# Attention with hashed buckets, then a channel mix: the same operations in another written sequence, on other engines

## The chip, the cores and the metric

The kernel runs on one core of a Trainium2 chip. The metric is the device time of one execution in microseconds (us). The engines are named as in the profile: PE is TensorE (matmuls; PEld its weight loads), DVE is VectorE, ACT is ScalarE, POOL is GpSimd and SP is SyncE, which here only issues transfers. Each engine works through its own queue in order and waits at semaphores for the others.

## The reference

```python
q_bits = (np.einsum('bhsd,dk->bhsk', q, proj) > 0)          # 6 sign bits for each row, k_bits alike
mask = q_bucket[:, :, :, None] == k_bucket[:, :, None, :]
scores = np.where(mask, scale * q @ k.T, -1e9)
attn = softmax(scores); x = attn @ v                        # 4 batches, 8 heads, 768 x 64
xk = mu_k * x + (1 - mu_k) * x_prev                         # x_prev: x shifted by one row; xr alike with mu_r
out = sigmoid(xr @ w_r) * (np.maximum(xk @ w_k, 0) ** 2 @ w_v)   # 512 -> 1024 -> 512
```
A row attends only to rows with the same six sign bits. The attention's output, 768 x 512 for each of four batches, goes through a gated feed-forward layer.

## The kernel before

Heads are taken in pairs: 16 pairs, numbered 0 to 15, four to a batch. In the names of operations the first number is the pair, `q` or `k` the side, and a further digit the head in the pair (0 or 1); `e` halves have one digit more.

For each pair: `ldq` loads q and k into `nat`, `ldv` loads v into `vn`. `hi` rounds q and k to fp16 (helper `scale_on`, L261 on ACT, L263 on DVE or POOL), `lo` computes what the rounding lost (L424, in the first pairs L482). `tr` transposes both by DMA (L428); pairs 0 and 1 are transposed on PE (`t`, L493) and copied out of PSUM by `evt` (L257). `bits` multiplies by the hash matrix (L448), `bx` keeps the signs as fp16 numbers (L451), and `row` copies these under the transposed q and k (L257), so that one matmul gives score plus matching bits. `sc` are the score matmuls (L566), nine steps of 1024 columns per pair; `exp` turns each into `pt` (L570, always on ACT). `va` and the three `vsum` steps (`vsum`, `b`, `c`; L379, L382, L385) prepare v and its sum over the rows. `oo` is the product with v (L593, in pairs 0 to 3 preceded by L588), `rc` and `ob` divide by the sum (L604 to L611), `ot` or `otd` transposes, `xt`, `xs`, `df` and `xk`, `xr` mix neighbouring rows (L657, L666).

Head 0 of pair 0 has a short path of its own (`add_prep_rows`): `y` transposes in fp32 on PE (L515), `ey` copies to SBUF on ACT (L257), four `hi0` roundings write q and k (two sides, two halves), `x` multiplies by the hash matrix in fp32 (L521), `ex` writes the signs (k side on ACT, L535; q side on DVE, L537).

After every fourth pair one batch of the second layer follows (`add_moe`): `kp` (L681), `relu` (L687 on ACT, L689 on DVE), `sq` (L692), `r` (L705) with `tanh` (L708), `v` (L718), `os` (L725) and the store `st`. The second layer of a batch is interleaved with the attention of later ones. Weights are loaded by `wl` and cast by `wc` (L257). `warm0` to `warm19` are matmuls on zeros (L280), and `nz` clears the rows under head 0's q and k.

All this makes 1332 operations, added in a fixed program order that gives each its dependencies. What sets the order in time is three lists at the top of the file. `ORDER` names the operations in the sequence in which their instructions are written, so it fixes the order of work inside each engine and the order of transfers on SP. `BANKS` gives each of 334 PSUM tiles its bank (eight halves of 2 KB, or four pairs for `sc` and `bits`). `ENGS` names the engine of each of the 229 operations that may run on more than one. The code only reads them:

```python
e = ENGS[self.flex] if ENGS else eng
self.slot = dict(zip(self.names, BANKS))
return [self.ops[i] for i in ORDER]
```

Of the kernel before, what the change touches and what calls it, by code (L numbers as in the profile page):

```python
# [17 lines left out]
    66, 71, 69, 1, 23, 67, 68, 22, 0, 32, 2, 29, 30, 26, 27, 24, 25, 81, 3, 4, 5, 6, 82, 31, 75, 76, 86, 84, 83, 114, 122, 88, 123, 85, 89,  # L18
    72, 87, 118, 93, 28, 33, 34, 35, 36, 37, 38, 39, 40, 41, 74, 77, 78, 79, 80, 95, 96, 99, 115, 126, 107, 70, 100, 108, 7, 8, 90, 91, 92,
    94, 97, 9, 101, 10, 11, 140, 124, 98, 102, 103, 12, 177, 119, 110, 141, 109, 127, 178, 170, 73, 171, 44, 120, 13, 179, 116, 136, 180,  # L20
    111, 104, 121, 138, 112, 137, 106, 105, 128, 181, 139, 117, 142, 129, 125, 148, 130, 230, 231, 143, 152, 149, 131, 113, 132, 134, 135,
    133, 233, 144, 234, 173, 174, 154, 155, 146, 153, 145, 147, 193, 14, 15, 156, 182, 226, 157, 205, 158, 150, 224, 223, 232, 172, 235,
    194, 206, 151, 183, 199, 45, 184, 186, 159, 203, 197, 200, 204, 276, 175, 201, 188, 283, 202, 176, 277, 185, 160, 161, 16, 187, 17, 162,
    163, 18, 189, 19, 20, 21, 279, 198, 227, 190, 191, 192, 242, 236, 284, 243, 195, 427, 426, 164, 212, 196, 237, 165, 228, 436, 437, 246,
    247, 248, 213, 249, 214, 250, 207, 244, 208, 209, 210, 251, 215, 256, 211, 216, 240, 238, 254, 229, 239, 166, 280, 245, 257, 252, 292,
    255, 285, 286, 217, 225, 491, 287, 253, 241, 218, 281, 282, 167, 42, 298, 288, 291, 290, 219, 293, 302, 169, 299, 304, 43, 168, 438,
    258, 52, 46, 48, 50, 303, 305, 278, 260, 265, 266, 261, 306, 262, 263, 220, 300, 264, 259, 439, 307, 301, 440, 296, 267, 308, 429, 289,
    441, 443, 492, 297, 47, 49, 442, 444, 309, 315, 294, 447, 316, 317, 493, 430, 268, 431, 269, 295, 449, 270, 448, 318, 319, 450, 271,
    453, 454, 445, 310, 457, 446, 432, 311, 312, 451, 459, 222, 272, 433, 273, 313, 434, 314, 458, 435, 452, 460, 463, 464, 461, 455, 465,
# [12 lines left out]
    752, 840, 896, 787, 755, 732, 407, 774, 1034, 639, 817, 812, 804, 905, 756, 805, 767, 806, 813, 768, 769, 807, 791, 414, 415, 775, 776,
    420, 820, 535, 810, 533, 793, 777, 895, 401, 792, 770, 794, 771, 800, 803, 802, 801, 821, 808, 421, 587, 588, 843, 852, 1035, 778, 842,
    811, 809, 416, 640, 641, 642, 643, 814, 815, 906, 844, 845, 422, 867, 417, 898, 907, 868, 863, 871, 423, 864, 418, 589, 424, 827, 652,
    828, 846, 847, 425, 872, 848, 897, 865, 1044, 866, 664, 653, 853, 849, 899, 654, 829, 649, 854, 665, 650, 830, 1045, 651, 655, 859, 860,
    831, 661, 861, 862, 646, 647, 656, 908, 648, 869, 877, 909, 779, 662, 887, 858, 900, 857, 856, 910, 590, 822, 870, 924, 878, 925, 928,
    879, 929, 644, 1037, 823, 824, 873, 874, 875, 658, 882, 876, 657, 880, 911, 1038, 855, 913, 881, 780, 825, 666, 1039, 1092, 1093, 920,
    667, 883, 826, 645, 663, 901, 673, 668, 669, 921, 926, 659, 674, 419, 1046, 884, 903, 927, 675, 679, 676, 677, 885, 886, 902, 930, 685,
    922, 680, 1047, 931, 923, 1090, 660, 833, 1089, 1036, 686, 687, 888, 413, 904, 1048, 1099, 781, 694, 670, 688, 671, 695, 681, 678, 689,
    672, 914, 691, 915, 1094, 1049, 1144, 1145, 912, 1052, 1051, 682, 692, 1065, 916, 1040, 937, 938, 683, 917, 918, 939, 1100, 1050, 1066,  # L50
    919, 1042, 1041, 782, 940, 690, 1043, 693, 684, 941, 832, 834, 835, 889, 696, 932, 1063, 933, 1055, 934, 1108, 1064, 1053, 1056, 836,
    935, 936, 697, 698, 1109, 1054, 700, 701, 1067, 1068, 1059, 1057, 708, 1101, 1091, 943, 1114, 1058, 702, 1102, 709, 1060, 1115, 783,
    784, 838, 837, 890, 891, 892, 944, 1151, 942, 945, 946, 1061, 1103, 1062, 1069, 703, 1112, 947, 953, 706, 1070, 1113, 707, 1124, 1152,
# [746 lines left out]
```

## Time and profile before

| | before |
|---|---|
| median of 3 runs | 246.6 us (246.0 to 246.65) |
| the profiled execution | 246.63 us, span 244.8 us |
| busy in the span | PE 231.4, DVE 202.3, ACT 183.9, POOL 77.6 us |
| costliest on ACT | 144 `exp` (L570), 139.2 us |
| costliest on DVE | 16 `lo` (L424), 26.6 us; 64 `sq` (L692), 23.6 us |
| costliest on POOL | 47 `row` copies (L257), 33.2 us |
| transfers | 43.98 MB, 180 GB/s on average |

The span is the time between the first and the last instruction of one execution; about 1.8 us lie around it. Busy time of one engine is the sum of its instructions. A matmul's end is modelled, so a busy PE can still have small gaps between starts. The number in brackets behind an idle time names who ended it.

### The profile page before, as it was taken

The page shows a single profiled execution, that of the slowest core. Times are in us where ns is not written, and L with a number is a line of the kernel's source. Part 1 is how long each engine was busy: PE and PEld are TensorE (multiplying, and loading weights), DVE is VectorE, ACT ScalarE, POOL GpSimd, SP SyncE. Part 2 cuts the span into 40 slices and gives each one's busy share as a digit, 9 for nine tenths or more (in the row PEclk, how much of TensorE's full clock was granted, in tenths as well). Part 3 has the DMA queues.
Part 4 walks back from the last instruction along what each step waited for, and adds up shares of the span by engine and source line. Part 5 has one row for each costly group of instructions (what it writes and reads, how often), then busy time and mean ns, then how long its engine had stood idle before and what let it go on. Part 6 is the DMA issues. An engine that isn't in the chain of part 4 may idle for free.

```text
span 244.8 us, 6181 instructions
## 1 busy us (share of the span) xinstructions
PE 231.4 (95%) x2472; PEld 140.2 (57%) x2472; DVE 202.3 (83%) x439; ACT 183.9 (75%) x231; POOL 77.6 (32%) x120
## 2 busy tenths in 40 slices
PE   3889799998999999999999999999999999999994
PEld 2345575665665666556557566457565674455443
DVE  2899999999998999899899999996577496677432
ACT  4799899997987999988978799785895962323321
POOL 5365458497944144213243333013010000000000
PEclk9999999999999999999999999999999999999999
DMA  7989999999899999999999458219201107121043
GB/s 219 378 199 239 250 233 172 295 276 347 312 180 241 290 326 254 222 310 248 250 258 195 108 143 176 51 54 206 75 3 32 47 0 119 45 86 43 3 171 131
DMA packets 72524, 43.98 MB, mean 180 GB/s; under 512 B 54832, under 2 KB 67504, under 8 KB 72496
## 3 DMA queue, kind: packets, MB, share of 16 engines
q1 hardware_dynamic: 72272, 43.40, 71.4%
q8 instruction: 19, 0.31, 0.5%
q10 hardware_dynamic: 224, 0.20, 0.3%
q14 instruction: 9, 0.07, 0.1%
HBM read 24.12 MB, written 6.29 MB: 124 GB/s over the span
## 4 chain that ended last, share of the span: by engine, by line
PE 71%; DVE 22%; issue 3%; ACT 1%; DMA 1%; DVEq 0%
PE ps_all L718 17%; PE ps_all L566 16%; PE ps_all L681 14%; PE ps_all L593 10%; PE ps_all L705 9%; DVE nh L424 3%; PE ps_all L448 3%; DVE a L257 3%; DVE bx L451 2%; DVE ob L611 2%; DVE xk L657 1%; DMA nat<-in_k_dram 1%; DVE k L692 1%; DVE nh L263 1%; DVE va L403 1%
## 5 line engine op out<-in xcount | busy, mean ns | idle before, releaser
L570 ACT ACTIVATE pt<-ps_all 128x1024 bf16<-128x1024 f32 x144 | 139.2, 1038 | 17.2 <-PE ps_all L566 16.2
L566 PE MATMUL ps_all<-a 128*128 128x256 f16 (+1 forms) x384 | 80.5, 325 | 3.1 <-DVE bx L451 0.9
L257 POOL COPY a<-bx 6x384 f32<-6x384 f32 x47 | 33.2, 706 | 67.3 <-DVE bx L451 44.2
L593 PEld LDWEIGHTS <-pt 128*128 128x128 bf16 x1152 | 43.6, 97 | 12.6 <-issue 4.2
L681 PE MATMUL ps_all<-xk,wk 128*128 128x384 bf16 x256 | 49.4, 326 | 0.4 <-DVE kr L689 0.4
L566 PEld LDWEIGHTS <-a 128*128 128x128 f16 x384 | 33.8, 97 | 25.3 <-issue 4.6
L593 PE MATMUL ps_all<-va,pt 128*128 128x65 bf16 x1152 | 46.2, 193 | 1.3 <-DVE xt L257 1.2
L718 PE MATMUL ps_all<-wv,k 128*128 128x512 bf16 (+2 forms) x208 | 47.2, 363 | 0.0
L681 PEld LDWEIGHTS <-wk 128*128 128x128 bf16 x256 | 24.1, 98 | 16.6 <-issue 1.4
L687 ACT ACTIVATE kr<-ps_all 128x384 bf16<-128x384 f32 x41 | 19.5, 500 | 16.0 <-PE ps_all L681 12.2
L718 PEld LDWEIGHTS <-k 128*128 128x128 bf16 x208 | 19.4, 98 | 19.3 <-issue 0.3
L708 ACT ACTIVATE rs<-ps_all 128x512 f32<-128x512 f32 x24 | 14.1, 600 | 18.5 <-PE ps_all L705 10.4
L692 DVE TENSOR_TENSOR k<-kr 128x384 bf16<-128x384 bf16 x64 | 23.6, 389 | 3.9 <-ACT kr L687 3.6
L424 DVE SCALAR_TENSOR_TENSOR nh<-nat,nh 128x1536 f16<-128x1536 f32 (+1 forms) x16 | 26.6, 1663 | 0.1
L725 DVE SCALAR_TENSOR_TENSOR os<-rs,ps_all 128x512 f32<-128x512 f32 (+2 forms) x26 | 16.7, 640 | 11.0 <-PE ps_all L718 10.2
L705 PE MATMUL ps_all<-wr,xr 128*128 128x512 bf16 x96 | 24.5, 379 | 0.0
L611 DVE TENSOR_TENSOR ob<-ps_all,rc 128x384 bf16<-128x384 f32 x32 | 17.4, 551 | 0.4
L451 DVE TENSOR_SCALAR bx<-ps_all 128x768 uint16<-128x768 uint16 (+1 forms) x16 | 15.2, 950 | 3.1 <-PE ps_all L448 3.0
L689 DVE TENSOR_SCALAR kr<-ps_all 128x384 bf16<-128x384 f32 x23 | 12.6, 549 | 4.9 <-PE ps_all L681 4.8
L403 DVE SCALAR_TENSOR_TENSOR va<-ps_all,vn 128x384 bf16<-128x384 f32 x24 | 12.5, 547 | 3.3 <-PE ps_all L398 2.2
L705 PEld LDWEIGHTS <-xr 128*128 128x128 bf16 x96 | 9.1, 98 | 9.4 <-issue 0.3
L448 PE MATMUL ps_all<-a,p 128*32 128x512 f16 (+1 forms) x248 | 13.3, 328 | 0.0
(90 smaller groups left out, 200.5 us busy)
## 6 DMA issues: line engine op xcount, KB each, us to landing
vn<-in_v_dram SPq DMA_DIRECT2D x16, 384.0 KB, 5.0
out_dram<-os SPq DMA_DIRECT2D x23, 256.0 KB, 2.2
nat<-in_q_dram SPq DMA_DIRECT2D x15, 384.0 KB, 5.0
nat<-in_k_dram SPq DMA_DIRECT2D x15, 384.0 KB, 5.2
wst<-in_moe_w_k_dram SPq DMA_DIRECT2D x2, 512.0 KB, 6.0
wst<-in_moe_w_r_dram SPq DMA_DIRECT2D x2, 512.0 KB, 5.4
wst<-in_moe_w_v_dram SPq DMA_DIRECT2D x2, 512.0 KB, 5.6
os<-in_moe_w_k_dram SPq DMA_DIRECT2D x1, 512.0 KB, 4.2
```

Source lines behind the costliest of these rows:

```text
L257: nc.scalar.copy(o, i_) if e == "ACT" else tt_on(e).tensor_copy(o, i_)
L424: nc.vector.scalar_tensor_tensor(out=nh[:, :, D:P], in0=nat.rearrange("p j (c d) -> p (j c) d", d=D), scalar=QS, in1=nh[:, :, 0:D], op0=AL ...
L448: nc.tensor.matmul(ps[32 * i : 32 * i + 32, lo:hi], w_, side_a[side][sa][:, j, lo:hi], start=st, stop=not st)
L451: nc.vector.tensor_scalar(out=bx_t[sx][0:rows].bitcast(U16), in0=ps_t[plan.slot[nm]][0:rows, 0:S].bitcast(U16).rearrange("p (c e) -> p c e ...
L566: nc.tensor.matmul(ps[:, lo - s * STEP : hi - s * STEP], side_a["k"][sa][:, j, jc * P : (jc + 1) * P], side_a["q"][sa][:, j, q0 : q0 + hi ...
L570: nc.scalar.activation(out=pt_t[sp][:, s * STEP : (s + 1) * STEP], in_=ps_t[plan.slot[nm]], func=AF.Exp, bias=EBIAS, scale=ESC)
L593: nc.tensor.matmul(oo[:, ic * 65 : ic * 65 + 65], pt_t[sp][:, o : o + P], va_t[sa][:, j, jc, 0 : D + 1], start=(not uc and ic == 0 and jc ...
L611: nc.vector.tensor_tensor(out=ob_t[so][:, :, j * D : (j + 1) * D], in0=oo[:, :, 0:D], in1=rc_t[sr][:, 1, :].unsqueeze(2).to_broadcast([P, ...
L681: nc.tensor.matmul(ps[:, 0:HALF], wk_sb[:, d, fc * P : (fc + 1) * P], xk_t[mx[d]][:, h * HALF : (h + 1) * HALF], start=(d == 0), stop=(d = ...
L692: nc.vector.tensor_tensor(out=k2_t[s2][:, h * HALF : (h + 1) * HALF], in0=kr_t[sk], in1=kr_t[sk], op=ALU.mult)
L705: nc.tensor.matmul(sm(nr), xr_t[mx[d]][:, c * P : (c + 1) * P], wr_sb[:, d, :], start=(d == 0), stop=(d == NDC - 1))
L718: nc.tensor.matmul(sm(nv)[:, x0:x1], k2_t[(b * NFC + fc) % NK2][:, c * P : (c + 1) * P], wv_sb[:, fc, x0:x1], start=(fc == 0), stop=(fc == ...
```

## The change

No operation is added, removed or resized. The three lists are replaced: `ORDER` by another permutation of the same 1332 numbers, `BANKS` differs in 156 of 334 places, `ENGS` in 80 of 229 places. The moves between engines are:

| operation | from | to | which |
|---|---|---|---|
| rounding of head 0 | POOL | ACT | `hi0q00` (so all four are on ACT) |
| `hi` | ACT | DVE | `hi1k0`, `hi9`, `hi11`, `hi14` |
| `evt` | DVE | ACT | `evt1k1` |
| `nz` | DVE | POOL | `nz0q0` |
| `va` | POOL | DVE | `va1`, `va2` |
| `vsum` | POOL to DVE, 13 | DVE to POOL, 10 | e.g. `vsum1`, `vsum6` with b and c to DVE; `vsum1c`, `vsum12` to POOL |
| `row` | POOL to DVE, 7 | DVE to POOL, 9 | e.g. `row1k1` to DVE; `row2q1`, `row2k1` to POOL |
| `relu` | ACT to DVE, 13 | DVE to ACT, 16 | |
| `wc` | | | `wc6` DVE to POOL, `wc7` POOL to ACT, `wc8` POOL to DVE |

In the first head the written sequence on each engine becomes:

| engine | before | after |
|---|---|---|
| PE | `warm0`, `y0k0`, `warm1` to `4`, `x0k0`, `y0q0`, two warm-ups, `x0q0` | `warm0` to `13`, `y0q0`, `y0k0`, `x0q0`, `x0k0` |
| ACT | `ey0k0`, `hi0k01`, `hi0k00`, `ex0k00`, `ey0q0`, `ex0k01`, `hi1k0`, `hi0q01`, `hi1k1`, `evt0q1`, `evt0k1`, `va0`, `exp0_2` | `ey0q0`, `hi0q01`, `ey0k0`, `hi0q00`, `hi0k00`, `hi0k01`, `ex0k00`, `hi1k1`, `ex0k01`, `evt0k1`, `evt0q1`, `exp0_2`, `va0` |
| DVE | `hi1q0`, `hi1q1`, `lo1q1`, `hi0q1`, `lo0q1`, `hi0k1`, `lo1q0`, `lo0k1`, `ex0q00`, `ex0q01` | `hi1q0`, `hi1q1`, `lo1q0`, `lo1q1`, `hi0k1`, `lo0k1`, `hi0q1`, `ex0q00`, `lo0q1`, `ex0q01` |

On SP the first loads stay in place; `ldv1` moves ahead of `ldq3`, `ldv2` from the ninth place behind the second `tr2`, `mur` from before `tr2` to behind `tr3`, and `ldv5` from before `tr6` to behind `wl7`. From 20 us on, neighbours change places on every engine by a few positions, in the last fifth by up to 19 positions on DVE. The bank of `oo0_1` was freed by `ob0` and is now one that `bx1` frees.

```diff
 ORDER = [
-    66, 71, 69, 1, 23, 67, 68, 22, 0, 32, 2, 29, 30, 26, 27, 24, 25, 81, 3, 4, 5, 6, 82, 31, 75, 76, 86, 84, 83, 114, 122, 88, 123, 85, 89,
+    1, 23, 29, 30, 26, 27, 24, 68, 25, 22, 28, 33, 34, 35, 36, 37, 0, 32, 38, 39, 31, 75, 76, 2, 3, 4, 5, 6, 7, 8, 9, 10, 11, 12, 13, 14,
+    15, 66, 71, 69, 67, 72, 107, 114, 122, 88, 115, 123, 99, 100, 81, 89, 93, 82, 91, 84, 90, 95, 92, 96, 94, 40, 41, 74, 77, 78, 79, 80,
...
 BANKS = [
-    3, 6, 0, 5, 2, 1, 7, 0, 6, 7, 2, 7, 3, 2, 0, 2, 2, 0, 3, 0, 0, 2, 2, 2, 6, 2, 2, 3, 2, 2, 0, 3, 3, 2, 3, 6, 7, 5, 0, 1, 0, 0, 1, 2, 0,
+    2, 6, 7, 7, 5, 1, 6, 0, 3, 2, 7, 6, 1, 2, 0, 2, 2, 0, 3, 3, 0, 2, 3, 2, 7, 2, 2, 3, 2, 2, 0, 3, 3, 0, 3, 6, 7, 1, 0, 1, 0, 0, 1, 2, 2,
...
 ENGS = [
-    "DVE", "DVE", "POOL", "POOL", "POOL", "POOL", "POOL", "POOL", "DVE", "POOL", "POOL", "ACT", "ACT", "ACT", "ACT", "ACT", "POOL", "ACT",
-    "DVE", "ACT", "DVE", "ACT", "POOL", "POOL", "ACT", "POOL", "POOL", "POOL", "DVE", "DVE", "ACT", "DVE", "DVE", "DVE", "ACT", "DVE",
+    "POOL", "DVE", "POOL", "POOL", "POOL", "POOL", "POOL", "POOL", "POOL", "ACT", "DVE", "ACT", "ACT", "ACT", "ACT", "ACT", "ACT", "ACT",
+    "DVE", "ACT", "DVE", "ACT", "POOL", "POOL", "ACT", "POOL", "POOL", "POOL", "DVE", "DVE", "DVE", "DVE", "DVE", "DVE", "ACT", "ACT",
...
```

22 lines of the change are left out of this document (11 added, 11 removed), and 115 rows, old and new, of tables (BANKS, ORDER).

## The prediction

> **What bounds the kernel now.** I read the page's busy shares first, then the busy time by stretch, then the chain that ended last, then the timeline where that chain changes engine.
>
> ```profile
> PE 231.4 (95%) x2472; PEld 140.2 (57%) x2472; DVE 202.3 (83%) x439; ACT 183.9 (75%) x231; POOL 77.6 (32%) x120
> ```
> ```profile
> 0.00:13.00 13.00, 8.32 (x47) 4.26 (x49) 7.55 (x19) 8.15 (x15) 5.25 (x31) 1.00 0.89 302
> 13.00:62.00 49.00, 44.49 (x655) 29.62 (x650) 47.95 (x78) 45.58 (x50) 33.31 (x37) 1.00 1.04 252
> 62.00:165.00 103.00, 101.98 (x1098) 61.91 (x1097) 98.52 (x218) 91.84 (x113) 35.61 (x47) 1.00 0.90 211
> 165.00:200.00 35.00, 35.00 (x432) 22.72 (x431) 22.72 (x66) 26.38 (x34) 3.45 (x6) 1.00 0.27 65
> ```
> The columns after the length are PE, PEld, DVE, ACT and POOL. The average of 95% on PE hides two regimes. From 13 to 62 us VectorE is busy 47.95 of 49 us, and PE has holes. From 62 us on PE is busy 101.98 of 103 us and then without a break, while VectorE still has 4.48 us free up to 165 us and a third of its time after that. So PE's order after 62 us can give nothing; what counts is when PE reaches the full stretch, and whether anything opens a hole in it. The chain says the same:
>
> ```profile
> 0.74 3.27 DMA nat<-in_k_dram
> 4.15 0.87 PE ps_all L515 x3
> 5.87 1.47 PE ps_all L521 x2
> ...
> 22.97 1.46 DVE nh L424
> ...
> 59.22 0.52 PE ps_all L593 x12
> 62.21 1.14 PE ps_all L681 x7
> ```
> It starts with a load and PE (the first head), is VectorE's from 14 to 59 us, and PE's afterwards. Three places of the timeline matter:
>
> ```profile
> 7.89 0.36 DVE L263 TENSOR_SCALAR nh<-nat 128x384 f16<-128x384 f32 x1 [1.01 <-DMA nat<-in_q_dram]
> 8.78 1.36 POOL L263 TENSOR_SCALAR a<-nh 64x384 f16<-64x384 f32 x1 [1.84 <-ACT nh L257]
> 25.18 0.33 PE L588 MATMUL ps_all<-vsu,tiny 128*128 128x390 bf16 x1 [0.71 <-DVE ob L611]
> ```
> VectorE stands 1.01 us for q of head 1 (`hi0q1`); GpSimd takes 1.36 us for one rounding; PE waits for `ob0` to free a bank.
>
> **Part 1, the first head (0 to 13 us).** In the new order VectorE does `lo1q0` and then head 1's k before it comes to `hi0q1`. It starts at 5.28 us as before (`pj` lands then, and no load ahead of it moved). Rows: two `pz` 0.35, `hi1q0` and `hi1q1` 0.63, `lo1q0` and `lo1q1` 2 x 0.55, `hi0k1` 0.36, `lo0k1` 0.55: that reaches 8.3 us, past the 7.89 us at which q landed. The 1.01 us of standing is filled: minus 1.0 us on the engine that bounds the next stretch. `nz0q0` (0.38 us) leaves VectorE before 5.28 us, where VectorE stood anyway, and goes to GpSimd, which stood until 5.25 us: zero; if that cover were gone, 0.4 us.
>
> The roundings. `hi0q00` leaves GpSimd (1.36) for ScalarE (0.52, L261's row for 64x384). All four now follow each other there with `ey` in front, so ScalarE's twelve steps before `exp0_2` are 2 x 0.48 + 4 x 0.52 + 2 x 0.48 + 0.52 + 2 x 0.80 = 6.1 us from 5.05 us, that is 11.2 us; the last thing that `sc0_2` reads, `ex0q01` on VectorE, would end near 10.3 us and PE needs 0.6 us. `exp0_2` began at 12.98 us with `va0` (0.84) ahead of it; now `va0` is behind it. So it comes about 1.8 us earlier, of which `va0` and `evt1k1` (0.80, new on ScalarE) take 1.64 back before head 1's exps. What remains for the rest is VectorE's 1.0 us.
>
> The warm-ups. Fourteen now stand ahead of the first transpose. In the trace those at 4.81 to 5.45 us follow each other at 0.21 us and later ones at 0.11 us; `x0k0`'s two matmuls start 0.69 us apart, `x0q0`'s 0.37. Fourteen at 0.21 are 3.0 us, from 1.19 to about 4.2 us, where PE stood for the load: zero, and 0.2 us if the load came sooner. [...]
>
> **Part 2, VectorE from 13 to 62 us.** Gained: `hi1k0` 0.36, `row1k1` and `row4q1` 2 x 0.45, `va1` and `va2` 2 x 0.51 (the 1024-wide cast took 0.68 on VectorE, times 0.75), `vsum1` 0.55, `vsum2c` and `vsum3c` 2 x 0.43 (130 wide): 3.7 us. Lost: `evt1k1` 0.54, `row2q1`, `row2k1`, `row3q1`, `row4q0` 4 x 0.45, `vsum1c` and `vsum2b` 2 x 0.43: 3.2 us. Net plus 0.5 us. The single `vsum1c` of before lasted 0.91 us, so the two gained could cost 1.0 us more: the net lies between 0 and 1.5, and I take 0.5 because the plain 130-wide sums (0.43) are nearer in shape to it. Of its 1.05 us idle VectorE may win back some: I take 0.3. Lead at 62 us: 1.0 - 0.5 + 0.3 = 0.8 us.
>
> Two smaller things. `oo0_1` now sits on a bank that `bx1` frees, not `ob0`, so the 0.71 us wait at 25.18 us goes; VectorE is next in line there, so I count none of it, at most 0.7 us. `hi7` (1.06) now stands before `xk3`; `xk3` ended 0.89 us before its first reader on PE, and that reader now comes behind `kp0_1_1` (first part) and `kp0_0_0`, with 0.3 us left over after VectorE's lead: zero, and up to 1.0 if the lead is missing.
>
> **Part 3, 62 to 165 us.** VectorE gains `hi9` and `hi11` (2 x 1.06), seven relus (0.55), four row copies (0.45), sums of `v` 3 x 0.55 + 2 x 0.36 + 4 x 0.41, a weight cast 0.68; it loses nine relus, four row copies, sums 2 x 0.55 + 2 x 0.36 + 2 x 0.41, a cast. Net 2.1 - 1.1 + 0 + 1.4 + 0 = plus 2.4 us, on 98.52 of 103 us: 100.9. ScalarE: plus two relus and a cast, minus two 1.50 us roundings: minus 1.0. GpSimd: some 3 us less. The cover for the 2.4 us is VectorE's 4.48 us of idle time, most of which are waits for PE or ScalarE that a later VectorE does not have: zero; the whole 2.4 if none of it covers.
>
> **Part 4, after 165 us.** VectorE and ScalarE have a third of their time free, PE's matmuls are the same, and the last of the three output pieces is 128 columns wide in both. Zero, and up to 0.5 either way, as one `os` row (0.64) more or less in front of `xk15` or the last store would make.
>
> **Queues.** SP issues the same transfers. `ldv2` falls from the ninth place to behind `tr2`, `ldv5` behind `wl7`; `ldq4q` and `ldq4k` stand among the `tr2`. A load took 5.0 us to land, and `va2`, `vsum5` and `bits2` come 7 us or more after their issue by the order: zero here, a rival below.
>
> **Sum** against the profiled execution (246.63 us, span 244.8 with 1.8 around it, the median of the runs is 246.6): 246.63 - 0.8 + 0 + 0 = 245.8 us. A measurement of this kernel can tell about 0.3%, 0.74 us, from no change.
>
> **Rivals.**
> A, the forecast: the lead survives. For it: VectorE's chain from 14 to 59 us. 244.9 to 245.9.
> B, the lead is eaten before 62 us (the sums cost 0.91, or ScalarE's waits on PE, 3.3 us in this stretch, do not shrink): 246.63 with 0.7 either side. For it: three engines are over 90% busy there.
> C, slower: VectorE becomes the bound between 62 and 165 us. PE reads VectorE's results just in time (`xk11` ended 0.28 us before `kp2_0_1`, `va5` 0.12 us before `oo5_1`). If none of the 2.4 us is covered: 246.63 - 0.8 + 2.4 = 248.2; it decides once less than 1.6 us is covered. Against it: the 4.48 us.
> D, slower: a late `v`. If `ldv5` behind `wl7`, which waits for the cast of `wc3`, holds GpSimd at `vsum5`, the `row6` copies queue behind it; they had 6 us to spare before `sc6_6`, so it takes more than 6 us of delay, and 1 to 2 us more would give 247.6.
> E, faster still: VectorE's operations get shorter because GpSimd does less. The squares (L692) last 0.35 us where GpSimd is idle and 0.60 where it is busy over half of them (51 and 10 cases, matched by time), which is 2.5 us of excess; L657 and L666 add some 4 us (0.60 and 0.63 against 1.07 and 0.91, 6 and 4 cases), and 3 of 35.6 us of GpSimd are a tenth: 0.6 us, 245.2. [...]
>
> **Chances.** A 0.32, E 0.08, B 0.20, C 0.30, D 0.10. Faster is A and E, 0.40; within 0.3% is B, 0.20; slower is C and D, 0.40. A is the likeliest single case, 245.8, with its own range of 244.9 to 245.9. Below, the 0.7 of the bank wait on top of the lead and some of E give 244.6; above, C with the dearer sums (248.2 + 1.0) gives 249.2: low 244.6, high 249.2.
>
> **What would show it.** Right: `hi0q1` without a DMA wait; `exp0_2` before 11.5 us; no wait on `ob` at `oo0_1`; the first L681 matmul between 61.0 and 61.5 us; PE idle after 62 us no more than the 1.0 us of before. Wrong: first L681 at 62 us or later (B); VectorE over 100.5 of 103 us and PE with new waits on L657, L666, L725 or L451 (C); GpSimd waiting for a `vn` load near 56 us (D).

## The result and the profile after

The changed kernel takes 247.26 us (median; 246.65 to 248.82), the kernel before 246.6 us beside it. The ratio is 1.0031, with an interval of 1.0017 to 1.0044: slower by 0.3%. Forecast were 245.8 us and a small gain. The profiled execution took 246.75 us, 0.5 us under the median, span 245.0 us; the span before was 244.8 us. Some executions of these kernels have a mean granted clock of 0.991 to 0.993 and take about 1.2 us longer than the others, which are called those at full clock; the medians hold both unless the text says otherwise.

First the busy shares, then the busy time by stretch; the columns after the length are PE, PEld, DVE, ACT and POOL:

```profile
PE 231.8 (95%) x2472; PEld 140.4 (57%) x2472; DVE 201.4 (82%) x441; ACT 183.8 (75%) x233; POOL 68.1 (28%) x116
```
```profile
0.00:13.00 13.00, 10.03 (x73) 6.28 (x74) 8.04 (x19) 9.29 (x16) 4.34 (x32) 1.00 0.86 295
13.00:62.00 49.00, 44.90 (x641) 29.35 (x640) 46.27 (x79) 47.12 (x52) 27.31 (x32) 1.00 1.08 267
62.00:165.00 103.00, 100.13 (x1092) 60.37 (x1090) 98.77 (x219) 88.09 (x111) 32.72 (x47) 1.00 0.90 206
165.00:200.00 35.00, 35.00 (x404) 22.23 (x402) 21.36 (x63) 26.06 (x33) 3.75 (x7) 1.00 0.27 69
```

Two things differ. From 13 to 62 us GpSimd has 6.0 us less to do and VectorE 1.7 us less, although VectorE got about as much work as it gave. From 62 to 165 us PE is busy 100.13 us instead of 101.98, while VectorE's sum there has hardly moved (98.77 against 98.52 us). That last comparison misleads, because the changed kernel enters this stretch further on in the program and leaves it about level. Counted from the first L681 matmul to 165 us, which is nearly the same work in both, VectorE is busy 101.10 us instead of 98.48 (the same view, the changed kernel first):

```profile
59.67:165.00 105.33, 102.46 (x1110) 61.74 (x1107) 101.10 (x221) 90.15 (x113) 32.72 (x47) 1.00 0.91 210
```
```profile
62.04:165.00 102.96, 101.94 (x1098) 61.88 (x1096) 98.48 (x218) 91.80 (x113) 35.57 (x47) 1.00 0.90 211
```

The start is better than forecast. These are the three places that the prediction showed (VectorE's, ScalarE's and PE's timeline), and the first L681 matmul:

```profile
8.10 0.35 DVE L263 TENSOR_SCALAR nh<-nat 128x384 f16<-128x384 f32 x1
```
```profile
5.54 0.52 ACT L261 ACTIVATE a<-nh 64x384 f16<-64x384 f32 x1
...
11.00 1.02 ACT L570 ACTIVATE pt<-ps_all 128x1024 bf16<-128x1024 f32 x1
```
```profile
23.63 0.33 PE L588 MATMUL ps_all<-vsu,tiny 128*128 128x390 bf16 x1
...
59.67 1.62 PE L681 MATMUL ps_all<-xk,wk 128*128 128x384 bf16 x9
```

`hi0q1` no longer waits for its load, `exp0_2` starts at 11.00 us instead of 12.98, `oo0_1` has no wait for `ob` in brackets, and the first L681 matmul comes at 59.67 us. In the profile of before it came at 62.04 us: PE has a lead of 2.4 us where 0.8 was forecast.

All of that lead is gone before the end. PE's idle time from 62 to 165 us shows two new waits (PE's timeline of the changed kernel, the time in brackets stood before the matmul):

```profile
79.16 0.65 PE L681 MATMUL ps_all<-xk,wk 128*128 128x384 bf16 x3 [1.11 <-DVE mc L410]
...
134.34 0.81 PE L681 MATMUL ps_all<-xk,wk 128*128 128x384 bf16 x4 [1.59 <-DVE ob L611]
```

The two largest of before, in the same view, were shorter and stood elsewhere:

```profile
76.65 0.59 PE L566 MATMUL ps_all<-a 128*128 128x512 f16 x2 [0.51 <-DVE bx L451]
...
137.47 1.46 PE L681 MATMUL ps_all<-xk,wk 128*128 128x384 bf16 x8 [0.36 <-DVE kr L689]
```

Neither new wait is for data. `kp0_4_1` needs the bank of `mean6`, which `mc6` frees; `kp1_3_1` needs the bank of `oo10_0`, which `ob10` frees. Both releases are late on VectorE. Matched operation by operation, PE's lead over the kernel before (median of eight microseconds each) is 2.4 us at 68 us, 2.9 at 76, 2.4 at 84, 1.6 at 92 and at 108, 1.4 at 116 and at 132, 0.4 at 140 and 0.2 at 148 us. Single values move by some tenths, because the two orders differ.

### The profile page after: what moved, and what is told of

Its sections match the earlier page's. It is cut to its first block, busy times and chain, and to the rows that moved or that the text cites. A ratio compares the mean times of both kernels' runs of the same rounds, so it can differ in the third digit from the quotient of the medians.

```text
span 245.0 us, 6174 instructions
## 1 busy us (share of the span) xinstructions
PE 231.8 (95%) x2472; PEld 140.4 (57%) x2472; DVE 201.4 (82%) x441; ACT 183.8 (75%) x233; POOL 68.1 (28%) x116
## 4 chain that ended last, share of the span: by engine, by line
PE 56%; DVE 26%; ACT 5%; issue 3%; DMA 2%; POOL 1%; SPq 1%; DVEq 0%; POOLq 0%; ACTq 0%
PE ps_all L718 15%; PE ps_all L566 12%; PE ps_all L681 11%; PE ps_all L705 8%; PE ps_all L593 7%; ACT pt L570 4%; DVE nh L424 3%; DVE k L692 3%; DVE bx L451 3%; PE ps_all L448 2%; DVE nh L263 2%; DMA muk<-in_moe_mu_k_dram 2%; DVE ob L611 2%; DVE va L403 2%; POOL a L257 1%
## 5 line engine op out<-in xcount | busy, mean ns | idle before, releaser
L681 PE MATMUL ps_all<-xk,wk 128*128 128x384 bf16 x256 | 48.2, 326 | 2.7 <-DVE ob L611 1.6
L257 POOL COPY a<-bx 6x384 f32<-6x384 f32 x49 | 34.1, 696 | 48.1 <-DVE bx L451 28.8
L681 PEld LDWEIGHTS <-wk 128*128 128x128 bf16 x256 | 24.3, 98 | 19.4 <-issue 4.2
L687 ACT ACTIVATE kr<-ps_all 128x384 bf16<-128x384 f32 x44 | 20.7, 494 | 16.9 <-PE ps_all L681 10.6
L692 DVE TENSOR_TENSOR k<-kr 128x384 bf16<-128x384 bf16 x64 | 24.6, 410 | 9.0 <-ACT kr L687 8.9
L424 DVE SCALAR_TENSOR_TENSOR nh<-nat,nh 128x1536 f16<-128x1536 f32 (+1 forms) x16 | 25.8, 1613 | 0.1
L611 DVE TENSOR_TENSOR ob<-ps_all,rc 128x384 bf16<-128x384 f32 x32 | 17.6, 551 | 0.4
L689 DVE TENSOR_SCALAR kr<-ps_all 128x384 bf16<-128x384 f32 x20 | 10.9, 550 | 3.3 <-PE ps_all L681 1.8
L448 PE MATMUL ps_all<-a,p 128*32 128x512 f16 (+1 forms) x248 | 13.3, 328 | 0.2 <-ACT pt L570 0.2
```

The source lines that it names most:

```text
L257: nc.scalar.copy(o, i_) if e == "ACT" else tt_on(e).tensor_copy(o, i_)
L424: nc.vector.scalar_tensor_tensor(out=nh[:, :, D:P], in0=nat.rearrange("p j (c d) -> p (j c) d", d=D), scalar=QS, in1=nh[:, :, 0:D], op0=AL ...
L611: nc.vector.tensor_tensor(out=ob_t[so][:, :, j * D : (j + 1) * D], in0=oo[:, :, 0:D], in1=rc_t[sr][:, 1, :].unsqueeze(2).to_broadcast([P, ...
L681: nc.tensor.matmul(ps[:, 0:HALF], wk_sb[:, d, fc * P : (fc + 1) * P], xk_t[mx[d]][:, h * HALF : (h + 1) * HALF], start=(d == 0), stop=(d = ...
L687: nc.scalar.activation(out=kr_t[sk], in_=i_, func=AF.Relu, scale=0.5 ** 0.5)
L692: nc.vector.tensor_tensor(out=k2_t[s2][:, h * HALF : (h + 1) * HALF], in0=kr_t[sk], in1=kr_t[sk], op=ALU.mult)
```

## The experiments

Theory 1 was that the order is at fault: two bank releases stand too late among VectorE's operations. Theory 2, the prediction's rival C in a milder form, was that VectorE as a whole bounds the stretch, so that a wait removed comes back at the next tile. Theory P came later: GpSimd's work beside them makes VectorE's operations longer. Medians are given with the ratio to the kernel before, run beside it; the changed kernel's own is 1.0031 (1.0017 to 1.0044).

### Which half of the change costs what

Order, banks and engines of one kernel up to the first L681 matmul, of the other for the rest:

```diff
-ORDER = changed
+ORDER = changed[:369] + [i for i in before if i not in changed[:369]]
...
```

> Order, banks and engines of the changed kernel up to the first L681 matmul (its first 369 operations), and those of the kernel before for the rest, in the order that the kernel before gives them. Theory 1: the changed start gives PE a lead of 2.2 us at the first L681 matmul, and the kernel before's rest has neither of the two late bank releases: the lead stays to the end but for some tenths, and the time is about 244.6 us (244.2 to 245.2), some 0.8% under the kernel before. Theory 2: what PE gains in the first 62 us VectorE can't follow in 62 to 165 us in either order: waits on VectorE appear there too, and the time is 246.0 to 247.0 us.

Measured: 245.55 us, ratio 0.9947 (0.992 to 0.9974).

```diff
-ORDER = changed
+ORDER = before[:375] + [i for i in changed if i not in before[:375]]
...
```

> The other way round: the kernel before up to its first L681 matmul (its first 375 operations), then order, banks and engines of the changed kernel. Theory 1: no lead at the first L681 matmul (62.0 us), and the changed rest costs the 2.7 us that it costs in the changed kernel: about 249.4 us (248.6 to 250). Theory 2: PE waits for VectorE in the rest only because it runs ahead of it; without the lead the waits on mc6 and ob10 shrink by what the lead was, and the time is 246.6 to 247.6 us.

Measured: 248.34 us, ratio 1.0084 (1.0053 to 1.0115).

The two fit each other: the changed start is worth 1.0 to 1.1 us (246.58 to 245.55, and 248.34 to 247.26), and the changed rest costs 1.7 to 1.8 us, with the lead and without it. So the changed rest is not slow only because PE runs ahead of VectorE in it; theory 2's numbers fail on both sides. Theory 1's sizes were too large on both. The first of the two is also the fastest version here that leaves no work out. Its profile (246.28 us, 0.7 us over its median) shows, though, that a lead is not safe in the rest of the kernel before either: PE is 2.3 us ahead at 62 us and 0.4 us from 76 us on. Four waits took the difference, two of them large (PE's timeline):

```profile
67.72 0.38 PE L566 MATMUL ps_all<-a 128*128 128x512 f16 x1 [0.72 <-ACT kr L687]
...
76.22 0.59 PE L566 MATMUL ps_all<-a 128*128 128x512 f16 x2 [1.03 <-DVE bx L451]
```

So the changed start's lead is worth 0.4 us at the end of this profile and 1.0 us by the medians, not the 2.4 us that stand at 62 us.

Further cuts were to find the place inside the rest.

> Order, banks and engines of the changed kernel for its first 735 operations (PE to about 117 us), then the kernel before. With the cut at 62 us the time was 245.55 us, with no cut (the changed kernel) 247.26 us: 1.7 us are lost somewhere behind 62 us. Theory 1 (late mc6 and its neighbours at 79 to 95 us, and late ob10 at 134 us, half each): about 246.4 us. If the stretch from 62 to 117 us costs nothing: 245.6 us. If all is lost there: 247.2 us.

> As the kernel cut at 117 us, with the cut behind 930 operations (PE to about 150 us), so that it holds the wait on ob10 at 134 us. Theory 1: all that is lost is lost before 150 us: 247.2 us, and 0.8 us over the kernel cut at 117 us. If the loss stands behind 150 us (the last batch and the tail): 245.6 to 246.4 us, no more than the kernel cut at 117 us.

Cut at 117 us: 245.87 us, 0.9969 (0.9941 to 0.9997). Cut at 150 us: 246.78 us, 1.0006 (0.9974 to 1.0038). By these, 0.3 us are lost from 62 to 117 us, 0.9 from 117 to 150 and 0.5 behind. Two more cuts show how far such numbers can be trusted:

> Order, banks and engines of the changed kernel for its first 461 operations (PE to 71 us), then the kernel before. The lead at 71 us is about 2.5 us. If the crossing keeps half of it or more: 244.8 to 245.4 us, and no wait on mc6 near 79 us. If the crossing costs what the one at 98 us cost (2.7 us of lead within 5 us): 246.6 to 247.2 us.

> Order, banks and engines of the changed kernel for its first 616 operations (PE to 98 us), then the kernel before. In the profiles the changed kernel's PE lead is 2.5 us at 92 us and 1.8 us at 100 us, and behind 100 us the kernel before's own order lost nothing in the kernels cut at 117 and 150 us. If the lead at the cut is kept: 244.8 us (1.8 under the kernel before). If the crossing costs what it cost at 62 us (2.3 to 0.4 us of lead) or at 117 us (1.3 to 0.3 us): 245.6 to 246.2 us.

Cut at 71 us: 246.38 us, 0.9981 (0.9952 to 1.0009). Cut at 98 us: 247.02 us, 1.0003 (0.9969 to 1.0037). Both are slower than the cuts at 62 and at 117 us (the cut at 71 us only by 0.1 to 0.4 us at full clock, where its median is 245.87 us and theirs are 245.51 and 245.74). In both the crossing itself opens a wait that neither kernel has (PE's timeline, one line of each, cut at 71 us first):

```profile
76.97 0.81 PE L681 MATMUL ps_all<-xk,wk 128*128 128x384 bf16 x4 [1.75 <-DVE ob L611]
```
```profile
102.63 0.22 PE L397 MATMUL ps_all<-vs,ones 128*128 128x128 bf16 x1 [0.97 <-DVE ob L611]
```

A cut locates a loss to about 1 us, no better. What the cuts show is the size of the whole rest. That the part with the wait on `ob10` is the largest piece fits PE's lead, which falls by 1.0 us from 132 to 140 us.

### The two waits, moved one at a time

```diff
 ORDER = [
...
-    520, 558, 603, 740, 369, 564, 372, 373, 521, 545,
+    545, 520, 558, 603, 740, 369, 564, 372, 373, 521,
...
```

> The changed kernel, with one VectorE instruction moved: mc6 (L410), which frees the PSUM bank of mean6, is written directly behind the second va6, ahead of hi9, the two sq0_5 and rc5. Theory 1 (the order alone: PE's lead of 2.2 us at the first L681 matmul is lost at two matmuls whose bank is freed late by VectorE, kp0_4_1 behind mc6 and kp1_3_1 behind ob10): PE's wait of 1.11 us on mc6 at kp0_4_1 (79.2 us) goes or falls under 0.3 us, PE is 1.0 us earlier from 80 us up to the wait on ob10, whose stretch is as before, and the time is about 246.3 us, 0.9 to 1.1 us under the changed kernel's. Theory 2 (VectorE, busy 98.8 of the 103 us from 62 to 165, is the bound there as a whole): the wait goes at kp0_4_1 but comes back at the next tile that VectorE frees, PE's lead at 114 us is the changed kernel's within 0.3 us, and the time is 247.2 +- 0.2 us.

Measured: 247.16 us, 1.0033 (1.0005 to 1.0061): nothing gained. The wait on `mc6` is gone, and two matmul groups later there is another one (PE's timeline of this kernel, whose profiled execution is 1.5 us late from about 40 us on):

```profile
81.31 0.52 PE L593 MATMUL ps_all<-va,pt 128*128 128x65 bf16 x12 [0.82 <-DVE ob L611]
```

At this place theory 2 is right: `ob5` stands behind the same squares and the same rounding (`hi9`), and is as late.

```diff
 ORDER = [
...
-    666, 590, 929, 873, 842, 1035, 1089, 425, 897, 1090, 1046, 824, 825, 924, 879, 880, 874, 875, 881,
+    929, 873, 842, 1035, 1089, 425, 897, 1090, 1046, 824, 825, 924, 879, 880, 874, 875, 881, 666, 590,
...
```

> The changed kernel, with two VectorE instructions moved: sq1_3 and xr6 are written behind ob10 (L611) instead of ahead of rc10, so that ob10 starts about 2 us earlier. Theory 1 (order): PE's wait of 1.59 us on ob10 at kp1_3_1 (134.3 us) falls to under 0.4 us, PE is 1.2 to 1.6 us earlier from 136 us on, and the time is about 245.9 us, 1.2 to 1.6 us under the changed kernel's. Theory 2 (VectorE as a whole bounds 62 to 165 us): what PE gains at 134 us is lost before 165 us to other VectorE waits, and the time is 247.2 +- 0.3 us.

Measured: 246.86 us, 1.0018 (0.9996 to 1.0039), 0.4 us under the changed kernel where theory 1 said 1.2 to 1.6. At full clock the median is 246.39 us against 247.2 us, so the order is worth 0.8 us, still less than theory 1 said. The 1.59 us are gone, and 0.58 us on `ob9` and 0.32 us on a relu follow at 137 us.

In `ENGS`, the places of `hi9` and `hi11`:

```diff
 ENGS = [
...
-    "DVE",
+    "ACT",
...
-    "DVE",
+    "ACT",
...
```

> The changed kernel with the roundings hi9 and hi11 back on ScalarE, at the same places of the order: VectorE has 1.9 us less to do from 62 to 165 us (two of 0.95 us), ScalarE 3.0 us more (two of 1.50 us). Theory 2 (VectorE's load bounds the stretch): most of the 1.9 us comes back, 245.6 to 246.3 us, and PE's waits on mc6 (1.11 us) and ob10 (1.59 us) both shrink. Theory 1 (order, not load): mc6 comes 0.95 us earlier and its wait falls to 0.2 us, the wait on ob10 stays within 0.3 us, and the time is 246.8 to 247.2 us. If ScalarE's 3.0 us more are not covered, its exps are late and the time is over 247.5 us.

Measured: 247.33 us, 1.0031 (1.0003 to 1.0059): the changed kernel's time. VectorE's busy time from 62 to 165 us fell by 2.0 us to 96.79, and PE's wait on `ob10` stayed at 1.59 us:

```profile
77.41 0.59 PE L566 MATMUL ps_all<-a 128*128 128x512 f16 x3 [0.83 <-ACT pt L570]
...
134.61 0.81 PE L681 MATMUL ps_all<-xk,wk 128*128 128x384 bf16 x4 [1.59 <-DVE ob L611]
```

Where `mc6` had held PE, `exp` now does: ScalarE has the two roundings, of 1.5 us each, in VectorE's place. That is against theory 2 as a statement on VectorE's load, as far as this run can tell: 2 us less of it bought nothing, and `ob10` came no earlier.

### What makes `ob10` late

VectorE's timeline ahead of `ob10` in the changed kernel, and GpSimd's beside it:

```profile
129.34 0.87 DVE L652 TENSOR_TENSOR df<-xt 128x768 bf16<-128x768 bf16 x1
...
130.19 0.59 DVE L692 TENSOR_TENSOR k<-kr 128x384 bf16<-128x384 bf16 x1
...
131.28 1.15 DVE L692 TENSOR_TENSOR k<-kr 128x384 bf16<-128x384 bf16 x1
132.36 0.77 DVE L666 TENSOR_TENSOR xr<-tm,xt 128x768 bf16<-128x768 f16 x1
...
133.72 0.56 DVE L611 TENSOR_TENSOR ob<-ps_all,rc 128x384 bf16<-128x384 f32 x1
```
```profile
128.74 2.40 POOL L257 COPY a<-bx 6x384 f32<-6x384 f32 x4 [2.26 <-issue]
131.22 1.00 POOL L379 TENSOR_TENSOR vt<-vn 128x384 f32<-128x384 f32 x1
132.30 0.41 POOL L382 TENSOR_TENSOR vt<-vt 128x128 f32<-128x128 f32 x1
132.79 0.60 POOL L385 TENSOR_TENSOR vs<-vt 128x128 bf16<-128x128 f32 x1
```

Two squares of the same shape take 0.59 and 1.15 us here and 0.35 us where GpSimd stands. In the kernel before VectorE does `row12q0` and `vsum12` itself at this place, and GpSimd stands for 4.25 us until that sum is there (VectorE's timeline of before, then GpSimd's):

```profile
130.47 0.35 DVE L257 COPY a<-bx 6x384 f32<-6x384 f32 x1
...
131.82 0.55 DVE L379 TENSOR_TENSOR vt<-vn 128x384 f32<-128x384 f32 x1
132.29 0.35 DVE L692 TENSOR_TENSOR k<-kr 128x384 bf16<-128x384 bf16 x1
```
```profile
132.52 0.41 POOL L382 TENSOR_TENSOR vt<-vt 128x128 f32<-128x128 f32 x1 [4.25 <-DVE vt L379]
```

The change moved both to GpSimd, and GpSimd's work now falls beside the squares. No run sets these two moves back alone. To test whether GpSimd's work stretches the squares, it was cut down at this place.

> The changed kernel with GpSimd's work from 128.7 to 133.4 us cut down: the copies row11q0, row12q0, row12k0 and row12k1 copy 8 of 384 columns, and the three sums of v of pair 12 take 2 of 64 columns, so the results of pairs 11 and 12 are not the reference's; everything else, the order too, is as in the changed kernel. Theory O (the order alone makes ob10 late): PE's wait on ob10 at kp1_3_1 stays at 1.3 us or more, and the time is 247.0 to 247.3 us. Theory P (the VectorE operations ahead of ob10 are late because GpSimd runs beside them: sq1_3 1.15 us against 0.35 us where GpSimd is idle, xr6 0.77 against 0.55, xka8 0.66 against 0.47, a square 0.59 against 0.35, together 1.45 us): the wait falls under 0.5 us and the time to 246.2 to 246.6 us.

Measured: 243.0 us, 0.9835 (0.9787 to 0.9883). The edit slipped: the full width was given in the wrong unit, so every other row copy of the kernel was halved too (192 of 384 columns), on GpSimd and on VectorE. It is no answer to its question, but it has a number of its own: GpSimd's busy time fell by 7.6 us (68.1 to 60.5), VectorE's by 6.9 us (201.4 to 194.5), of which the 13 copies that VectorE does itself explain 1.7, and the kernel became 4.3 us faster. Made again with the other copies whole, so that only copies of pairs 11 and 12 and the sums of pair 12 leave work out:

```diff
-        E = D + 1 if uc else D
+        E = D + 1 if uc else 2 if n == 12 else D
...
-            def row(e, i=i, side=side, j=j):
-                copy_on(e, side_a[side][sa][D : D + NB, j, :].bitcast(FP32), bx_t[sx][32 * i : 32 * i + NB, :].bitcast(FP32))
+            def row(e, i=i, side=side, j=j, W=16 if (n, side, j) in ((11, 'q', 0), (12, 'q', 0), (12, 'k', 0), (12, 'k', 1)) else S):
+                copy_on(e, side_a[side][sa][D : D + NB, j, 0:W].bitcast(FP32), bx_t[sx][32 * i : 32 * i + NB, 0:W].bitcast(FP32))
```

> The changed kernel with GpSimd's work from 128.7 to 133.4 us cut down, and this time only that: the copies row11q0, row12q0, row12k0 and row12k1 copy 8 of 384 columns, the three sums of v of pair 12 take 2 of 64 columns (so the results of pairs 11 and 12 are not the reference's); all other row copies have their 384 columns. Up to 128 us the trace is the changed kernel's. Theory O (order alone): PE's wait on ob10 at kp1_3_1 stays at 1.3 us or more, time 247.0 to 247.3 us. Theory P (stretching by GpSimd): sq1_3 takes under 0.6 us instead of 1.15, the wait falls under 0.5 us, PE is 1.1 to 1.5 us earlier at 140 us, and the time is 245.8 to 246.5 us.

Measured: 245.2 us, 0.9935 (0.9905 to 0.9966), 2.0 us under the changed kernel with the order untouched. VectorE's timeline, then PE's:

```profile
129.21 0.56 DVE L652 TENSOR_TENSOR df<-xt 128x768 bf16<-128x768 bf16 x1
...
129.75 0.35 DVE L692 TENSOR_TENSOR k<-kr 128x384 bf16<-128x384 bf16 x1
...
130.41 0.37 DVE L692 TENSOR_TENSOR k<-kr 128x384 bf16<-128x384 bf16 x1
130.70 0.55 DVE L666 TENSOR_TENSOR xr<-tm,xt 128x768 bf16<-128x768 f16 x1
...
131.94 0.56 DVE L611 TENSOR_TENSOR ob<-ps_all,rc 128x384 bf16<-128x384 f32 x1
```
```profile
132.40 0.53 PE L593 MATMUL ps_all<-va,pt 128*128 128x65 bf16 x12
132.76 0.81 PE L681 MATMUL ps_all<-xk,wk 128*128 128x384 bf16 x4
```

The square takes 0.37 us, `ob10` starts 1.8 us earlier, and the wait at `kp1_3_1` is gone. PE is 1.6 us earlier from `kp1_3_1` to the end; nothing takes it back. So theory P holds at this place: in this order `ob10` is late because GpSimd works beside it, and theory 2 is out there. The two squares shrank (1.15 to 0.37 and 0.59 to 0.35 us), and so did `df` (0.87 to 0.56) and `xr` (0.77 to 0.55); `ob` with its input in PSUM is 0.56 us in both. `xs` and `xka`, with one tensor input each, shrank too, by 0.31 and 0.19 us. By what means GpSimd's work stretches them is not shown.

The same without leaving work out: three of the copies go to VectorE, behind the operation that PE waits for (910, 912 and 913 are `row12q0`, `row12k0` and `row12k1`).

```diff
 ORDER = [
...
-    910, 913, 832, 648, 781, 666, 590,
+    832, 648, 781, 666, 590,
...
-    663, 826, 667, 925, 782, 876, 855, 912,
+    663, 826, 910, 912, 913, 667, 925, 782, 876, 855,
...
 ENGS = [
...
-    "POOL",
+    "DVE",
...
-    "POOL", "POOL",
+    "DVE", "DVE",
...
```

> The changed kernel with row12q0, row12k0 and row12k1 on VectorE instead of GpSimd, written directly behind the ob9 that follows ob10; nothing is left out. VectorE has 3 x 0.35 = 1.05 us more to do, all behind ob10; GpSimd has three copies of 0.5 us less from 128.7 to 131.2 us, its row11q0 and vsum12 come earlier by as much. Theory P (stretching): at least half of the 1.45 us by which the operations ahead of ob10 were stretched goes, PE's wait on ob10 falls from 1.59 to 0.3 to 0.9 us, and the time is 246.2 to 246.9 us. Theory 2 (VectorE's load is what counts): the 1.05 us more come back on PE before 165 us, and the time is 247.3 us or more.

Measured: 246.32 us, 0.9995 (0.9973 to 1.0016), 0.9 us under the changed kernel although VectorE does more. At full clock it is 246.23 us, so by its time alone it is hardly told from `ob10_early` (246.39 us); what it shows is that `ob10` can come early without being moved in the order. The copies, three in 1.08 us, follow `ob9` (VectorE's timeline), and `kp1_3_1` has no wait over 0.2 us; two waits of 0.45 us on `bx` at 129 us and 0.35 us on a relu at 136 us are new:

```profile
132.22 0.56 DVE L611 TENSOR_TENSOR ob<-ps_all,rc 128x384 bf16<-128x384 f32 x1
132.69 0.51 DVE L692 TENSOR_TENSOR k<-kr 128x384 bf16<-128x384 bf16 x1
133.12 0.54 DVE L611 TENSOR_TENSOR ob<-ps_all,rc 128x384 bf16<-128x384 f32 x1
133.70 1.08 DVE L257 COPY a<-bx 6x384 f32<-6x384 f32 x3
```

Both edits together do not add up:

```diff
 ORDER = [
...
-    910, 913, 832, 648, 781, 666, 590,
+    832, 648, 781,
...
-    875, 881, 658, 882, 663, 826, 667, 925, 782, 876, 855, 912,
+    875, 881, 666, 590, 658, 882, 663, 826, 910, 912, 913, 667, 925, 782, 876, 855,
...
```

> As rows12_on_dve, and also sq1_3 and xr6 behind ob10, as in ob10_early (246.39 us in its executions at full clock). Theory P: no wait over 0.3 us on ob10 or ob9, 245.6 to 246.2 us, as far under the changed kernel as the cut-down GpSimd work brought. Theory 2: no better than ob10_early, 246.4 to 247.2 us.

Measured: 246.96 us, 1.0025 (1.0009 to 1.0041). With the operations ahead of it unstretched, `ob10` gains nothing by being moved forward (it starts at 132.28 us, against 132.22 with the first edit alone); what was moved behind it now delays the relus instead (PE's timeline):

```profile
136.74 2.76 PE L681 MATMUL ps_all<-xk,wk 128*128 128x384 bf16 x16 [1.14 <-DVE kr L689]
```

### Where the lead of the start comes from

```diff
-ORDER = changed
+ORDER = changed[:100] + [i for i in before if i not in changed[:100]]
...
```

> The changed kernel's first 100 operations (the first head, the warm-ups, bits and score matmuls of the first 14 us), then the kernel before. The changed kernel up to the first L681 matmul, followed by the kernel before, took 1.0 us less than the kernel before. Theory S (all of this gain is the first head's): about 245.6 us, VectorE 1.0 to 1.5 us earlier from 14 us to 60 us. Theory P (the gain needs the engine moves of 13 to 62 us, which take 6 us off GpSimd and shorten VectorE's SBUF-to-SBUF operations beside it): PE is 0.8 us earlier at 18 us, VectorE's operations from 13 to 62 us keep the lengths of before, the lead at the first L681 matmul is under 1 us, and the time is 246.0 to 246.6 us.

Measured: 245.9 us, 0.9978 (0.9954 to 1.0001). PE is 0.9 us ahead at 14 us and 0.6 us ahead from 76 us to the end. That is the forecast's Part 1 by itself, near the 0.8 us forecast for the whole. The rest of the 2.4 us at 62 us comes from elsewhere; the place is PE's wait for a bank at `oo0_1`, which this kernel still has:

```profile
24.41 0.33 PE L588 MATMUL ps_all<-vsu,tiny 128*128 128x390 bf16 x1 [0.77 <-DVE ob L611]
...
29.39 0.59 PE L566 MATMUL ps_all<-a 128*128 128x512 f16 x3 [0.82 <-DVE ob L611]
```

So the bank was set back in the changed kernel, with `rc0` and `ob0` of head 0 written ahead of `hi4` so that they free it as early as they can:

```diff
 ORDER = [
...
-    283, 151, 199, 200, 159, 203, 204, 426, 235, 160, 201, 161, 157, 226, 158,
+    157, 158, 283, 151, 199, 200, 159, 203, 204, 426, 235, 160, 201, 161, 226,
...
 BANKS = [
-    2, 6, 7, 7, 5, 1, 6, 0, 3, 2, 7, 6, 1, 2, 0, 2, 2, 0, 3, 3, 0, 2, 3, 2,
+    2, 6, 7, 7, 5, 1, 6, 0, 3, 2, 7, 6, 1, 2, 0, 2, 2, 0, 3, 3, 0, 2, 3, 3,
...
```

> The changed kernel with oo0_1 again on a bank that ob0 frees (that of oo0_0), as in the kernel before, and rc0 and ob0 of head 0 written ahead of hi4 so that they come no later than they can. If the bank is what gave the lead beyond the first head's: PE waits about 1.2 us on ob0 at oo0_1 (23.6 us in the changed kernel), the lead at the first L681 matmul falls from 2.2 us to 1.0 to 1.4 us, and the time is 247.0 to 248.0 us (the rest eats a lead, so little of it need show). If the bank is worth nothing, as the forecast's Part 2 counted it: the lead stays within 0.3 us of 2.2 us.

Measured: 248.17 us, 1.0043 (1.0017 to 1.0069).

```profile
25.14 0.33 PE L588 MATMUL ps_all<-vsu,tiny 128*128 128x390 bf16 x1 [1.17 <-DVE ob L611]
```

PE is 1.4 us later than in the changed kernel from 28 us to the end. In the traces the bank was worth 1.2 to 1.4 us of the 2.4, and this loss, too, is carried unchanged through the changed rest, so a lead made at the start is not eaten there as such. Over all executions the difference is smaller: 0.9 us between the medians, 0.3 us by the ratios.

In `ENGS`, the places of `va1`, `vsum1` and `va2`:

```diff
 ENGS = [
...
-    "DVE", "DVE",
+    "POOL", "POOL",
...
-    "DVE",
+    "POOL",
...
```

> The changed kernel with va1, va2 and vsum1 back on GpSimd (where the kernel before has them), at the same places of the order. VectorE has three operations less (0.56 + 0.76 + 0.56 = 1.88 us) between 20 and 26 us, GpSimd three more (about 0.83 + 1.15 + 0.85 us). Theory L (own lengths alone count, as the forecast's Part 2 did): VectorE is up to 1.9 us earlier from 27 us on, and PE reaches the first L681 matmul at 59 us or before. Theory P (GpSimd's work stretches VectorE's SBUF-to-SBUF operations beside it: lo3 took 1.46 us in the kernel before, 0.95 here): hi3 and lo3 go back to about 1.1 and 1.46 us, VectorE's gain is at most 0.8 us, and the chain through GpSimd (va, then vsum) is later, so that the first L681 matmul comes at 59.8 us or later, up to 61.5. Time: 246.8 to 247.6 us by both, since the stretch behind 62 us takes back a lead.

Measured: 246.9 us, 1.0018 (0.9985 to 1.0051), between the two kernels and not told from either. VectorE gives 1.88 us of work away; from 19 to 30 us others of its operations take 1.2 us more (four row copies 2.05 us together instead of 1.49, `lo4` 2.30 instead of 1.86, `vsum1b` 0.45 instead of 0.28). The stretched operations are others than those named in advance, `hi3` and `lo3` kept 0.56 and 0.96 us, but the sum is as theory P has it: PE's distance to the changed kernel does not move (1.0 us at 12 us, ahead of the moved operations, and 1.1 us at 60 us; this execution has a mean granted clock of 0.993, and its eight matmuls of L448 at 13 us take 1.27 us where they take 0.83 in the changed kernel).

```diff
 ENGS = [
...
-    "ACT",
+    "POOL",
...
```

> The changed kernel with one engine set back: hi0q00 on GpSimd (1.36 us there, 0.52 us on ScalarE). GpSimd has nothing else to do from 5.5 us on; ey0q0 ends at 5.5 us, so hi0q00 would end by 7.0 us, ahead of sc0_2 at 10.4 us, and ScalarE's queue is 0.5 us shorter. By the forecast's reading of the first head (ex0q01 on VectorE is the last input of sc0_2) exp0_2 starts at 11.0 +- 0.2 us and the time stays at 247.2 +- 0.3 us: the part that names the change is worth nothing by itself. If it matters, exp0_2 moves by 0.5 us or more, either way, and the time with it.

`exp0_2` starts at 11.10 us, so moving this rounding to ScalarE is worth nothing by itself. The time was 248.26 us, 1.0035 (1.0011 to 1.0058). The median at full clock is 247.4 us, against 247.2 us of the changed kernel.

```diff
 ORDER = [
...
-    2, 3, 4, 5, 6, 7, 8, 9, 10, 11, 12, 13, 14, 15, 66, 71, 69, 67, 72, 107, 114, 122, 88,
+    2, 66, 71, 69, 67, 72, 107, 114, 122, 88,
...
-    40, 41, 74, 77, 78, 79, 80, 83,
+    40, 41, 74, 77, 78, 79, 80, 83, 3, 4, 5, 6, 7, 8, 9, 10, 11, 12, 13, 14, 15,
...
```

> The changed kernel with 13 of the 14 warm-up matmuls ahead of y0q0 moved behind x0k0: one warm-up, then y0q0 and y0k0. By the forecast's Part 1 they are worth nothing: the four matmul groups of the first head take up to 0.9 us longer (y0 0.87 us each and x0 1.4 us a pair, the rows of the kernel before), VectorE comes to ex0q00 only at 8.5 us and ScalarE to ex0k00 at 7.9 us, so that exp0_2 starts at 11.0 to 11.3 us and the time is 247.2 +- 0.3 us. If the warm-ups matter: exp0_2 at 11.8 us or later and the time 0.5 us or more up. A second reading: the granted clock. Of the executions with the new start 18 of 103 had a mean clock of 0.991 to 0.993 and were about 1.2 us longer, with the old start 1 of some 40; if the block of warm-ups does that, none of these executions should have it.

Measured: 247.57 us, 1.0031 (0.9996 to 1.0065). Without the warm-ups in front the four `x0` matmuls take 2.05 us together instead of 1.46. `exp0_2` starts at 11.90 us, 0.9 us late, because the transposes of head 1's q and k, and with them ScalarE's copies out of PSUM, stand behind the moved warm-ups; yet PE is only 0.2 us later from 20 to 76 us. VectorE's queue, not the first `exp`, sets the pace there, as Part 1 had it.

## Why the prediction was wrong, point by point

**Part 1** was right. The wait at `hi0q1` is filled, `exp0_2` starts at 11.00 us (11.2 forecast), the warm-ups are hidden. The first head alone moved PE by 0.9 us and the end by 0.6 to 0.8.

**Part 2** had two sizes wrong, both too small. The bank wait at `oo0_1`, 0.71 us in the row, was counted as nothing because VectorE was thought next in line; set back, it costs 1.2 to 1.4 us to the end in the traces and 0.9 us in the medians. And VectorE's operations were costed by their own lengths, plus 0.5 us net. The moves came to about zero (3.5 us gained, 3.7 us lost), and the operations that VectorE does in both kernels became 2.5 us shorter in sum over the first 62 us, beside 6.0 us less work on GpSimd from 13 to 62 us. Rival E named this mechanism at 0.6 us. `v_prep_on_pool` shows the rate at one place: 1.88 us of VectorE work given to GpSimd, 1.2 us of stretching taken back.

**Part 3** is the step that failed. It set VectorE's 2.4 us of added work at zero, since "VectorE's 4.48 us of idle time" would cover it. The 2.4 us themselves were about right, although the sum left out `hi14` (0.95 us): from the first L681 matmul to 165 us VectorE is busy 2.6 us longer. What was wrong is to take an idle sum for a cover. The changed rest costs 1.7 to 1.8 us where zero was forecast, and the loss sits in single operations that free a bank and come late; an idle sum says nothing on those. At the largest, `ob10`, the lateness is GpSimd's work falling beside the six operations ahead of it (0.30, 0.31, 0.24, 0.19, 0.78 and 0.22 us longer than with that work cut down): 2.0 us of stretching, 1.59 us of PE waiting, 1.6 us at the end of the trace. Rival C had the stretch and the direction right, but not the mechanism: 2 us less VectorE work (and 2 us more on ScalarE in that stretch) changed nothing, and the new waits are on L410 and L611, not on the lines that C named. Rival E's mechanism was counted only as a gain; placed badly, it is a loss, and no rival said that. From 62 to 165 us GpSimd has 2.9 us less to do, and yet the operations that VectorE does there in both kernels take 1.5 us more in sum, not 0.6 us less.

In medians the start gave 1.0 to 1.1 us, where 0.8 us was forecast, and the rest took 1.7 to 1.8 us: 246.6 - 1.05 + 1.75 = 247.3 us.

**Part 4 and the queues** are not shown wrong. The cuts leave 0.5 us behind 150 us, inside their uncertainty.

The signs listed under "what would show it" were right for the start, and the last two failed: the first L681 matmul came before the range (59.67 us against 61.0 to 61.5), and PE was idle 2.87 us from 62 to 165 us instead of 1.0. None of the signs named for a wrong forecast appeared.

Open: whether the squares ahead of `mc6` (two in 1.67 us) are stretched to the point of causing that wait was not tried; only its removal by order was, and the next release took its place. So of the two new waits only the one on `ob10` has its cause shown. Where the 0.5 us behind 150 us go was not followed.

## What to carry to other kernels

Price a reordering not by an engine's idle sum but by the few operations that free a buffer for the bound engine: list what stands ahead of each in the new order, and what the other engines do at that moment. Where one engine's work stretches another's, as GpSimd's here made one square of VectorE last 1.15 us instead of 0.37, moving an operation between them is worth its length minus the stretch that it starts, or plus the stretch that it stops. Here that came to near zero at one place (`v_prep_on_pool`), and to 0.9 us gained by giving VectorE more work at another (`rows12_on_dve`). When a wait vanishes from the profile, ask whether another one stands behind it. For the one at `oo0_1` there was none: in the traces it makes up 1.2 to 1.4 of the 1.6 us by which the lead at 62 us was forecast too small.

## What the runs showed of the hardware

In these runs GpSimd's work lengthens VectorE's operations, and by how much depends on what falls beside it. In the changed kernel the squares take 0.35 us in the mean where GpSimd is idle (47 cases) and 0.63 us where it is busy over half of them (14 cases). With 7.6 us less of its work in the same order (`pool_light_at_130`) VectorE's busy time fell by 5.2 us beyond its own halved copies. The changed kernel has 9.5 us less of it than the kernel before (68.1 against 77.6 us), otherwise placed, and the operations that both do on VectorE are only 1.3 us shorter in sum. In the changed kernel squares take 0.32 to 1.18 us; in the kernel before `xk` and `xr` of L657 take 1.00 to 1.75 us. In both kernels `bx` keeps 0.94 to 0.96 us (16 cases each) and `ob` 0.51 to 0.56 us (32 cases each); the mean of `ob` is 0.55 us where GpSimd is idle and where it is busy over half of them.

In some executions the granted clock fell after the start. With fourteen warm-ups in a block ahead of the first transpose, 38 of 203 executions had a mean granted clock between 0.991 and 0.993 and took about 1.2 us more; with the kernel before's start it was 4 of 156. That the block does it is not shown. With the block moved behind the first matmuls it was 0 of 12, but `oo0_1_bank_back`, which has the block in place, has 0 of 12 too. On the chip on which the block was moved, the other kernels that have it show 4 of 30 and the kernel before 3 of 29. In three profiled ones the clock is low for some microseconds between 8 and 20 us: 0.80 and 0.77 from 8 to 16 us in `mc6_early`, 0.63 from 16 to 20 us in `hi0q00_on_pool`, 0.58 there in `ob10_early` (PE's busy time by stretch of the last; the columns are the length, PE, the granted clock and the DMA's):

```profile
13.00:16.00 3.00, 1.66 (x14) 1.00 1.17 303
16.00:20.00 4.00, 3.52 (x24) 0.58 1.08 258
20.00:25.00 5.00, 4.71 (x69) 0.99 1.03 191
```

Why it fell in these executions and not in the others no run shows.
